# Sums, turns and products of a fused attention and highway layer, moved into two 64-row halves of the array

## The chip, the cores and the metric

The kernel runs on one core of a Trainium2 chip. The core has a matrix engine (TensorE, PE in the profile), VectorE (DVE), ScalarE (ACT), GpSimd (POOL) and SyncE (SP), which here only issues transfers; 16 DMA engines move data between HBM and the on-chip memory SBUF. TensorE writes its results into PSUM, eight banks of 512 fp32 columns on 128 partitions; VectorE and ScalarE read and write PSUM, GpSimd works on SBUF alone. The metric is the device time of one launch in microseconds: a median of 118.66 us over two runs (118.6 and 118.73) for the kernel before.

## The reference

q, k and v have the shape 8 batches x 8 heads x 576 positions x 64. Per batch and head

    q_s = exp(q) / sum of exp(q) over the 64 features      (per position)
    k_s = exp(k) / sum of exp(k) over the 576 positions    (per feature)
    x   = q_s @ (k_s^T @ v)                                (576 x 64)

The maxima that the reference takes off before exp cancel in the quotients. The eight heads side by side make x a matrix of 4608 rows and 512 columns, and a highway layer follows:

    H   = max(x @ w_h, 0)
    T   = 1 / (1 + exp(-(x @ w_t + b_t)))
    out = T * H + (1 - T) * x

## The kernel before

**Tiles.** The output is made in 36 tiles of 128 rows. Of each two batches b and b+1 come nine: four tiles of b, four of b+1, and one that holds the last 64 rows of both (tiles 8, 17, 26 and 35). Tiles 0, 4 and 5 are worked in two halves of the heads (HALVED); tile 35 is the last (LAST), its gate is split into two pieces of 256 columns.

**Order of the work.** ORDER (line 16) is one list of steps, written out by hand, such as `xu_9_0` or `bw_7:A`. The loop at the end goes through it and calls one function for each step. Every engine runs its own instructions in the order of the list, and semaphores hold an instruction until its inputs are there and its buffer is free. A letter names the engine: A for ScalarE, D for VectorE, P for GpSimd; F is an exp over a whole batch. Loads and stores are issued on SP's queue, in the order of the list too; a load waits until its landing buffer (three for each of q, k, v) is free.

**Steps of a batch.** `k`, `v`, `q` load. `ek` and `eq` are the exp of k and q on ScalarE, `vc` the cast of v to fp16. `kv` (line 262) multiplies exp(k) with v in 64 x 64 pieces of the array, 72 matmuls of 65 columns for a pair of head groups; the 65th column is the sum of exp(k). `kr` takes its reciprocal, and `kn` (line 283) writes the normed product to kvb, two heads on the diagonal of a 128 x 130 block, zeros beside them, and a column of ones for each head, from which the sum over exp(q) comes. `qt` (line 310) turns exp(q) on TensorE in three groups, 8, 8 and 2 turns of 128 x 128, and `qc` copies them to SBUF; for batch 7 a DMA (`qd`) turns the two large groups.

**Steps of a tile.**

- `xu` (line 348): four matmuls of 130 columns with kvb give x before its division, and the sums of exp(q). For a tile of two batches they are eight, each on 64 columns of the array.
- `rs`, `x` (lines 367, 372): VectorE takes the reciprocals and divides.
- `xt` (line 379), `xe`: TensorE turns x in four turns of 128 x 128, VectorE or ScalarE copies it to SBUF.
- `bw` (line 394): the bias b_t goes into a PSUM bank of the gate, by a copy on ScalarE (A) or by a matmul with ones (no letter).
- `mt` (line 406), `mh` (line 414): four matmuls of 512 columns each, with w_t into the gate's bank and with half of w_h less the identity into the carry's bank.
- `th`: tanh of half the gate, on ScalarE. `dd`: VectorE takes max(-x/2, carry). `uu`: (tanh + 1) times that, on VectorE, or with P in two steps on GpSimd; then tanh writes to SBUF (LIFTED) and the gate's bank is free after it. `oo`: adds x, on GpSimd. `st`: stores.

The identity taken from w_h and the halves make this equal to T * H + (1 - T) * x.

**PSUM.** Two banks for gates (ps_t), two for carries (ps_g), two for xu and kv together (ps_x), one for qt (ps_q), one for xt and the filling matmuls at the start (ps_xt).

Of the kernel before, what the change touches and what calls it, by code (L numbers as in the profile page):

```python
# [18 lines left out]
w_t_2 kr_0_0 whd_0:P whd_2:P w_t_0 k_1_2 v_1_2 q_1_0 k_1_0 v_1_0 fill_5 q_1_4 kn_0_0 q_2_0 k_2_0 eq_0_2 xu_0_0 v_2_0  # L19
q_3_0 rs_0_0 whc_0:A x_0_0 k_3_0 fill_4 v_3_0 kv_0_1 fill_3 kr_0_1 kn_0_1 xu_0_1 rs_0_1 xu_1_0 rs_1_0 qt_0_1 x_1_0  # L20
fill_6 whd_3:P qc_0_1 xt_1_0 xu_3_0 qt_0_2 qc_0_2:A xe_1_0:D fill_1 rs_3_0 x_3_0 x_0_1 xt_3_0 xu_2_0 rs_2_0 x_2_0
wtc_2:P whc_2:A mh_1_0 wtc_0:P vc_1_3 ek_1_3 ek_1_2 vc_1_0 xe_3_0:D mh_3_0 dd_1 xt_0_1 xt_0_0 mt_1_0 xe_0_0:D mh_0_0
xe_0_1 dd_3 xt_2_0 mh_0_1 mt_0_1 th_1_0 xe_2_0:D dd_0 vc_1_2:A kv_1_1 uu_1_0 oo_1_0 eq_1_0 mt_0_0 th_0_0 ek_1_0 ek_1_1
kr_1_1 bw_3 qt_1_0 vc_1_1:A kn_1_1 qc_1_0 mt_3_0 xu_5_1 uu_0_0 mh_2_0 th_3_0 bw_2 rs_5_1 x_5_1 dd_2 xu_4_1 kv_1_0
kr_1_0 eq_1_1 rs_4_1 xt_5_1 mt_2_0 th_2_0 kn_1_0 bw_5 xe_5_1:D x_4_1 xu_5_0 mt_5_1 qt_1_1 eq_1_2 rs_5_0 x_5_0 xt_5_0
xu_4_0 bw_4:A uu_3_0:P oo_3_0 xe_5_0:D mh_5_1 rs_4_0 x_4_0 mh_5_0 xt_4_1 qc_1_1:A xt_4_0 xe_4_1:D dd_5 eq_2_0 xe_4_0:D
v_4_0 mt_5_0 th_5_0 xu_6_0 qt_1_2 rs_6_0 qc_1_2 oo_0_0 mt_4_1 mh_4_1 mh_4_0 uu_2_0:P x_6_0 mt_4_0 eq_2_1 xt_6_0 xu_8_0
uu_5_0 bw_6:A xe_6_0:D qt_2_0 rs_8_0 x_8_0 mh_6_0 oo_5_0 th_4_0 xt_8_0 dd_4 uu_4_0 xu_7_0 mt_6_0 ek_2_0:F rs_7_0
vc_2_2:A bw_8 xe_8_0:D mt_8_0 x_7_0 th_6_0 xt_7_0 th_8_0 oo_2_0 vc_2_0 kv_2_0 oo_4_0 qc_2_0 q_4_0 bw_7:A qt_2_1
qc_2_1:A dd_6 uu_6_0:P oo_6_0 eq_3_0:F xe_7_0:D kr_2_0 kn_2_0 mh_8_0 xu_9_0 rs_9_0 x_9_0 mt_7_0 th_7_0 bw_9 dd_8  # L30
uu_8_0:P qt_2_2 qc_2_2:A xu_10_0 bw_10:A xt_9_0 xe_9_0:D rs_10_0 x_10_0 ek_3_0 mh_7_0 dd_7 ek_3_2 mh_9_0 xu_12_0 k_4_0
xt_10_0 k_5_0 rs_12_0 qt_3_0 xe_10_0:D x_12_0 mt_9_0 th_9_0 uu_7_0:P q_4_9 dd_9 xu_11_0 qc_3_0 vc_3_2:A xt_12_0
mt_10_0 rs_11_0 mh_10_0 x_11_0 v_5_0 q_5_0 vc_3_0 st_1_1 q_5_9 uu_9_0 dd_10 oo_7_0 kv_3_0 qt_3_1 th_10_0 oo_8_0 st_1_0
xe_12_0 bw_12:A mh_12_0 kr_3_0 qc_3_1:A kn_3_0 xu_14_0 rs_14_0 x_14_0 bw_11:A xt_11_0 xe_11_0 mt_12_0 th_12_0 qt_3_2
v_6_0 xt_14_0 oo_9_0 k_6_0 xu_13_0 q_6_0 xe_14_0 mh_11_0 dd_12 qc_3_2 mt_11_0 rs_13_0 eq_4_0:F th_11_0 uu_12_0
uu_10_0:P x_13_0 dd_11 xu_15_0 rs_15_0 vc_4_0 mh_14_0 x_15_0 st_5_1 dd_14 qt_4_0 oo_10_0 vc_4_2 xu_16_0 rs_16_0 x_16_0
xt_13_0 xe_13_0:D oo_12_0 bw_14:A bw_13:A ek_4_0:F st_3_0 mt_14_0 th_14_0 xu_17_0 rs_17_0 bw_15:A x_17_0 qc_4_0
xt_15_0 mt_13_0 kv_4_0 xe_15_0:D kr_4_0 uu_11_0:P oo_11_0 th_13_0 qt_4_1 uu_14_0:P st_3_1 mh_13_0 vc_5_2 xt_16_0
kn_4_0 mh_15_0 xe_16_0:D vc_5_0 xu_18_0 ek_5_0:F dd_13 xt_17_0 qc_4_1:A uu_13_0 xe_17_0:D dd_15 rs_18_0 oo_14_0
bw_16:A mt_15_0 mh_16_0 x_18_0 th_15_0 uu_15_0:P mt_16_0 dd_16 mh_17_0 oo_13_0 bw_17:A th_16_0 oo_15_0 kv_5_0 uu_16_0  # L40
kr_5_0 kn_5_0 oo_16_0 eq_4_2 dd_17 qt_4_2 xt_18_0 eq_5_0 mt_17_0 st_5_0 xe_18_0 xu_20_0 rs_20_0 mh_18_0 qc_4_2:A
bw_18:A q_7_0 th_17_0 mt_18_0 eq_5_1 bw_20:A uu_17_0:P x_20_0 xt_20_0 dd_18 vc_6_2 xe_20_0:D xu_21_0 th_18_0 rs_21_0
# [23 lines left out]
def kernel(  # L66
# [40 lines left out]
    b32 = consts.tile([P, DM], FP32, name="b32")  # L107
# [28 lines left out]
    def halves(b, k):  # L136
        return (k, k + 1) if b < 2 else (0, 2)
# [396 lines left out]
```

## Time and profile before

| | |
|---|---|
| median of the runs | 118.66 us |
| profiled execution, first to last instruction (span) | 116.9 us |
| TensorE busy | 109.5 us (94%), granted clock 0.995 |
| VectorE busy | 93.3 us (80%) |
| ScalarE busy | 90.0 us (77%) |
| GpSimd busy | 89.1 us (76%) |
| moved by DMA | 40.58 MB, 347 GB/s over the span |

The profile is of one execution. Of its time outside the span nothing is recorded; the median of the runs, 118.66 us, lies 1.8 us above the span, and that is taken for what lies around it. Busy time counts an engine's own instructions. Matmuls are pipelined, and their recorded ends are modelled, so what a matmul costs in a row is read from start to start. A group of instructions has a line of the kernel (L361 is line 361), an engine, what it writes and reads, the piece of the array in rows x columns for TensorE (128*64), the shape, its count, its busy time in us and the mean of one in ns. PEld is the loading of weights, which overlaps the matmuls.

### The profile page before, as it was taken

What the parts mean: (1) busy time and instruction counts of PE and PEld (TensorE: products, weight loads), DVE (VectorE), ACT (ScalarE), POOL (GpSimd) and SP (SyncE); (2) the same over time, 40 slices, a digit from 0 to 9 for tenths busy, and PEclk for the clock granted to TensorE, in tenths of its full rate; (3) what the DMA queues carried; (4) which work ended last, traced back from release to release, by engine and by line L of the source; (5) the groups of instructions that cost most, each with busy time, mean ns of one, the idle gap of its engine ahead of it and who ended that gap; (6) DMA issues with size and microseconds to landing.
All of it is one profiled execution on the core that took longest, in us unless ns stands there. A gap on an engine that the chain in (4) does not pass through costs nothing.

```text
span 116.9 us, 3424 instructions
## 1 busy us (share of the span) xinstructions
PE 109.5 (94%) x1351; PEld 61.6 (53%) x1351; DVE 93.3 (80%) x222; ACT 90.0 (77%) x132; POOL 89.1 (76%) x99
## 2 busy tenths in 40 slices
PE   5999987999999999999999999999999999999930
PEld 2354544545665656565665547566564555554520
DVE  5642587589799979979889798988989887899870
ACT  4356461897999999989999999998597998545520
POOL 5022237208996999999999999999989699999960
PEclk9999999999999999999999999999999999999998
DMA  2999999999999999999999999999999956992875
GB/s 42 399 392 377 408 398 385 375 377 379 393 391 397 383 391 393 358 375 387 357 376 360 387 392 363 390 381 383 399 398 217 302 204 270 397 404 115 315 295 179
DMA packets 24195, 40.58 MB, mean 347 GB/s; under 512 B 5362, under 2 KB 11762, under 8 KB 24180
## 3 DMA queue, kind: packets, MB, share of 16 engines
q1 hardware_dynamic: 24032, 40.24, 96.9%
q8 instruction: 10, 0.16, 0.6%
q10 hardware_dynamic: 148, 0.14, 0.4%
q14 instruction: 5, 0.04, 0.1%
HBM read 30.41 MB, written 9.44 MB: 341 GB/s over the span
## 4 chain that ended last, share of the span: by engine, by line
PE 67%; POOL 15%; issue 6%; DVE 5%; DMA 3%; SPq 1%; POOLq 0%; DVEq 0%
PE tps L411 18%; PE gps L419 16%; PE turned L167 9%; POOL o L471 7%; PE xu L361 6%; PE turned L384 5%; PE kv L269 5%; PE qps L324 4%; POOL u L451 4%; DMA out_dram<-o 3%; POOL g L450 2%; PE qps L319 2%; POOL v L259 2%; DVE x L376 2%; PE tps L401 1%
## 5 line engine op out<-in xcount | busy, mean ns | idle before, releaser
L471 POOL TENSOR_TENSOR o<-u,x 128x512 f32<-128x512 f16 (+1 forms) x36 | 40.6, 1143 | 1.6 <-DVE u L453 0.7
L411 PE MATMUL tps<-w16t,xT 128*128 128x512 f16 (+1 forms) x148 | 37.3, 373 | 0.0
L419 PE MATMUL gps<-w16h,xT 128*128 128x512 f16 x144 | 36.8, 379 | 0.5 <-DVE xT L391 0.5
L376 DVE TENSOR_TENSOR x<-xu,rs 128x512 f16<-128x512 f32 (+1 forms) x39 | 25.2, 649 | 2.4
L259 POOL CAST v<-v 128x1152 f16<-128x1152 f32 (+1 forms) x14 | 14.0, 1010 | 14.7 <-DMA v<-in_v_dram 13.7
L439 DVE SCALAR_TENSOR_TENSOR d<-x,gps 128x512 f16<-128x512 f16 x36 | 24.5, 680 | 0.3
L451 POOL TENSOR_TENSOR u<-g,d 128x512 f16<-128x512 f16 x17 | 19.7, 1158 | 1.7 <-DVE rs L370 0.4
L253 ACT ACTIVATE ek<-k 128x576 f16<-128x576 f32 (+2 forms) x15 | 17.9, 1225 | 3.0 <-DMA k<-in_k_dram 3.0
L419 PEld LDWEIGHTS <-xT 128*128 128x128 f16 x144 | 13.0, 98 | 12.3 <-DVE xT L391 1.8
L399 ACT COPY tps<-ball 128x512 f32<-128x512 f32 x28 | 16.6, 597 | 3.5 <-DVE u L453 3.2
L411 PEld LDWEIGHTS <-xT 128*128 128x128 f16 x148 | 13.2, 98 | 10.6 <-DVE xT L391 0.4
L361 PE MATMUL xu<-kvb,eq 128*128 128x130 f16 (+1 forms) x160 | 14.8, 224 | 0.2 <-DVE kvb L287 0.2
L384 PE MATMUL turned<-idh,x 128*128 128x128 f16 x144 | 14.2, 220 | 0.5 <-DVE x L376 0.5
L391 DVE COPY xT<-turned 128x512 f16<-128x512 f16 (+1 forms) x28 | 10.9, 391 | 4.2 <-PE turned L384 3.0
L435 ACT ACTIVATE tps<-tps 128x512 f32<-128x512 f32 (+1 forms) x20 | 11.2, 559 | 3.6 <-PE tps L411 3.3
L453 DVE SCALAR_TENSOR_TENSOR u<-tps,d 128x512 f16<-128x512 f32 (+1 forms) x19 | 12.7, 671 | 1.4 <-ACT tps L435 0.6
L361 PEld LDWEIGHTS <-eq 128*128 128x128 f16 (+1 forms) x160 | 10.0, 100 | 7.3 <-DVE x L376 2.5
L167 PE MATMUL turned<-blank 128*128 128x512 f16 x40 | 12.4, 458 | 1.5 <-POOL blank L149 1.3
L384 PEld LDWEIGHTS <-x 128*128 128x128 f16 x144 | 9.8, 98 | 6.0 <-DVE x L376 2.1
L307 ACT ACTIVATE qe<-q 128x1024 f16<-128x1024 f32 (+3 forms) x9 | 9.4, 1052 | 4.1 <-DMA q<-in_q_dram 4.1
L450 POOL TENSOR_SCALAR g<-th 128x512 f16<-128x512 f16 x17 | 10.6, 621 | 0.9 <-ACT th L433 0.9
L433 ACT ACTIVATE th<-tps 128x512 f16<-128x512 f32 x17 | 10.0, 594 | 0.9 <-PE tps L411 0.9
(48 smaller groups left out, 106.8 us busy)
## 6 DMA issues: line engine op xcount, KB each, us to landing
k<-in_k_dram SPq DMA_DIRECT2D x6, 1152.0 KB, 12.2
v<-in_v_dram SPq DMA_DIRECT2D x6, 1152.0 KB, 12.0
out_dram<-o SPq DMA_DIRECT2D x23, 256.0 KB, 4.0
q<-in_q_dram SPq DMA_DIRECT2D x10, 512.0 KB, 11.5
out_dram<-o SPq DMA_DIRECT2D x6, 512.0 KB, 3.8
k<-in_k_dram SPq DMA_DIRECT2D x4, 576.0 KB, 9.3
q<-in_q_dram SPq DMA_DIRECT2D x2, 1152.0 KB, 14.2
q<-in_q_dram SPq DMA_DIRECT2D x2, 640.0 KB, 10.5
```

What stands on the lines that cost most here:

```text
L167: nc.tensor.matmul(spare, blank[:, 0:P], blank, start=True, stop=True, skip_group_check=True)
L253: nc.scalar.activation(t[:, :, c:c + n].rearrange("p j c d -> p c j d"), T[f"k32{b}"][:, c:c + n].rearrange("p c (j d) -> p c j d", j=NJ), ...
L259: copy(v16[b % NV][:, c:c + n, :, 0:D], T[f"v32{b}"][:, c:c + n].rearrange("p c (j d) -> p c j d", j=NJ))
L361: nc.tensor.matmul(dst, turned_q(b, jp, n), kvb[b % NKV][:, hh, kk], start=True, stop=True, skip_group_check=True)
L376: nc.vector.tensor_mul(t[:, k0:k1], sums(i, k)[:, :, :, 0:64], T[f"rs{i}_{k}"][:, 0:k1 - k0].unsqueeze(3).to_broadcast([P, k1 - k0, 4, D]))
L384: nc.tensor.matmul(t[:, n], T[f"x{i}"][:, n0 + n % 2:n0 + 2 * P:2], idh, is_transpose=True, start=True, stop=True, skip_group_check=True)
L399: nc.scalar.copy(t[:, cs], ball[:, cs])
L411: nc.tensor.matmul(T[gate(i, k)][:, cs], T[f"xT{i}"][:, n], w16["t"][:, n, cs], start=False, stop=(n == parts[-1] and not first), skip_gro ...
L419: nc.tensor.matmul(t, T[f"xT{i}"][:, n], w16["h"][:, n], start=(first and n == parts[0]), stop=(n == parts[-1] and not (first and len(part ...
L439: nc.vector.scalar_tensor_tensor(t, T[f"x{i}"], -0.5, T[f"gps{i}"], op0=ALU.mult, op1=ALU.max)
L451: nc.gpsimd.tensor_mul(t, g, T[f"d{i}"])
L471: eng.tensor_add(t[:, cs], T[f"u{i}_{h}"][:, cs], T[f"x{i}"][:, cs])
```

## The change

From tile 9 on, and for q from batch 3 on, TensorE works in two halves of 64 rows, the upper with its own weights and its own PSUM bank, the lower likewise.

- `xu`: eight matmuls of 64 rows and 65 columns, one for each head, in place of four with zeros in half of the block. The normed product goes to kvl, without zeros; `kn` is then one instruction. A tile of two batches has sixteen.
- `xt` and `qt`: 64 x 64 identities, eight and sixteen (or four) turns of 64 rows and 64 columns, halves in different banks.
- `mm_i_0` and `mm_i_1` replace `mt` and `mh` of tiles 9 to 34: the gate's product is in one half of the array while the carry's is in the other, eight matmuls of 64 rows and 512 columns each; the second step swaps the halves. A drain of TensorE stands ahead of the second, as both halves add up in the same two banks.
- PSUM: xu, kv, qt and xt share two pairs of banks, given out by the order of the list.
- `bw` has a third form (D), a copy by VectorE.
- ORDER is new from its third line on. GpSimd has 24 `uu` (17 before), VectorE nine `bw` (none), ScalarE 22 `bw` (28), TensorE six (nine). Of the casts of v, ScalarE has ten (five), VectorE four (one), GpSimd six (fourteen). VectorE has 16 `qc` (10), ScalarE six (12); of `xe` VectorE has 26 (28), ScalarE 13 (11). Loads and stores are the same, in another order.

The diff, cut:

```diff
 ORDER = """
...
-kr_5_0 kn_5_0 oo_16_0 eq_4_2 dd_17 qt_4_2 xt_18_0 eq_5_0 mt_17_0 st_5_0 xe_18_0 xu_20_0 rs_20_0 mh_18_0 qc_4_2:A
-bw_18:A q_7_0 th_17_0 mt_18_0 eq_5_1 bw_20:A uu_17_0:P x_20_0 xt_20_0 dd_18 vc_6_2 xe_20_0:D xu_21_0 th_18_0 rs_21_0
...
+vc_5_0:A rs_20_0 x_20_0 mm_18_1 xu_21_0 rs_21_0 dd_18 th_18_0 mm_19_0 ek_6_0:F uu_17_0:P oo_17_0 x_21_0 xt_20_0
...
+xt_22_0 v_6_0 xe_22_0 mm_21_0 mm_21_1 uu_20_0 bw_22:A xu_24_0 x_23_0 dd_21 th_21_0 bw_23:D xt_23_0 st_16_0 eq_4_2
...
+dd_22 oo_18_0 xe_24_0:D mm_23_1 st_12_1 rs_25_0 q_7_0 x_25_0 kv_6_0 qt_4_2 th_22_0 dd_23 bw_24:A th_23_0 mm_24_0
+kr_6_0 kn_6_0 uu_23_0 qc_4_2:A xu_30_0 q_7_9 rs_30_0 eq_7_1 st_12_0 xt_25_0 xe_25_0:D mm_24_1 st_8_0 v_7_0 qt_6_0
...
+xu_27_0 mm_25_1 oo_22_0 xe_30_0 rs_27_0 x_27_0 xu_26_0 xt_27_0 rs_26_0 th_25_0 k_7_0 mm_30_0 xe_27_0:D xu_29_0 oo_23_0
...
+xu_28_0 dd_30 rs_29_0 x_29_0 ek_7_0:F mm_26_0 qd_7_0 st_23_0 xt_29_0 dd_27 xe_29_0:D uu_24_0:P rs_28_0 oo_25_0 eq_6_2
...
 """
...
-    ps_x = pool("ps_x", 1, space=PS)
-    ps_q = pool("ps_q", 1, space=PS)
-    ps_xt = pool("ps_xt", 1, space=PS)
+    ps_s = pool("ps_s", 1, space=PS)
...
-    kvb = [consts.tile([P, 2, 2, 130], FP16, name=f"kvb{i}") for i in range(NKV)]
+    kvb = [consts.tile([P, 2, 2, 130], FP16, name=f"kvb{i}") for i in range(2)]
+    kvl = [consts.tile([P, 2, 2, 66], FP16, name=f"kvl{i}") for i in range(NKV)]
...
+    EARLY, EARLY_Q = 9, 3
...
+    users = [pair_user(s) for s in ORDER.split()]
+    final = {u: n for n, u in enumerate(users) if u}
+    PAIR, held = {}, [None, None]
+    for now, u in enumerate(users):
+        if u and u not in PAIR:
+            free = [n for n in range(2) if held[n] is None or final[held[n]] < now]
+            PAIR[u] = min(free, key=lambda n: -1 if held[n] is None else final[held[n]])
+            held[PAIR[u]] = u
+    space = [ps_s.tile([P, 2, DM], FP32, tag=f"s{i}", name=f"space{i}") for i in range(2)]
+    space = {u: space[n] for u, n in PAIR.items()}
+    spare = space["early"][:, 1]
...
+    def setup_late(e):
+        for i in range(NKV):
+            nc.gpsimd.memset(kvl[i][:, :, :, 0::65], 1.0)
...
-        ps = once(f"kvps{b}", lambda: ps_x.tile([P, 2, DM], FP32, tag="xu", name=f"kv_{b}"))
+        ps = T[f"kvps{b}"] = space[f"kv{b}"]
...
+        if b >= 2:
+            nc.vector.tensor_mul(kvl[b % NKV][:, :, :, 1:65], kv_of(b, k)[:, :, :, 0:64],
+                                 T[f"rz{b}_{k}"].unsqueeze(3).to_broadcast([P, 2, 2, 64]))
+            return
...
+    def qt_late(e, b, g):
+        t = T[f"qps{b}_{g}"] = space[f"qt{b}_{g}"].bitcast(FP16)
+        for n in range(8 if g < 2 else 2):
+            for r in range(2):
+                rows = slice(64 * r, 64 * r + 64)
+                dst = t[:, r, 64 * n:64 * n + 64]
+                if g == 2:
+                    src = T[f"qe{b}"][rows, 8, 2 * n:2 * n + 2].rearrange("p c d -> p (c d)")
+                elif b in WIDE:
+                    main = T[f"qe{b}"].rearrange("p j c d -> p (j c d)")[:, 0:MAIN]
+                    main = main.rearrange("p (hh j kk f) -> p j hh kk f", j=4, hh=2, kk=2)
+                    src = main[rows, 2 * g + n // 4, n % 2, n % 4 // 2]
+                else:
+                    src = T[f"qe{b}"][rows, 4 * g + n // 2, n % 2 * 2:n % 2 * 2 + 2].rearrange("p c d -> p (c d)")
+                    dst = t[:, r, 0:512].rearrange("p (a k t s u) -> p a k s t u", a=2, k=2, s=2, u=2)[:, n // 2 % 2, n % 2, n // 4]
+                nc.tensor.matmul(dst, src, idh[rows, rows], is_transpose=True, start=True, stop=True,
+                                 skip_group_check=True)
...
-        t = T[f"qps{b}_{g}"] = ps_q.tile([P, a, 4, s * NP], FP16, tag="qps", name=f"qps_{b}_{g}")
-        if b in WIDE and g < 2:
...
+        if b >= EARLY_Q:
+            qt_late(e, b, g)
+            return
+        t = T[f"qps{b}_{g}"] = space["early"][:, 0].bitcast(FP16)[:, 0:a * 4 * s * NP].rearrange("p (a n t) -> p a n t", a=a, n=4)
...
-        copy(t.rearrange("p a n t -> p (a n t)"), T[f"qps{b}_{g}"].rearrange("p a n t -> p (a n t)"))
         T[f"eq{b}_{g}"] = t
+        if b < EARLY_Q:
+            copy(t.rearrange("p a n t -> p (a n t)"), T[f"qps{b}_{g}"].rearrange("p a n t -> p (a n t)"))
+        elif b in WIDE and g < 2:
+            copy(t.rearrange("p a n (r t) -> p r (a n) t", r=2),
+                 T[f"qps{b}_{g}"][:, :, 0:DM].rearrange("p r (m t) -> p r m t", m=8))
+        else:
+            m = 4 if g < 2 else 2
+            copy(t.rearrange("p a (k r) t -> p r (a k) t", r=2),
+                 T[f"qps{b}_{g}"][:, :, 0:m * s * NP].rearrange("p r (m t) -> p r m t", m=m))
...
-            t = ps_x.tile([P, 2, DM], FP32, tag="xu", name=f"xu_{i}")
+            t = space[f"xu{i}"]
...
+        if i >= EARLY:
+            for n in range(4):
+                kk, hh = n // 2, n % 2
+                for a, b in enumerate(bs):
+                    for w in range(2):
+                        part = slice(64 * w, 64 * w + 64)
+                        rows = slice(0, P) if len(bs) == 1 else slice(64 * a, 64 * a + 64)
+                        nc.tensor.matmul(t[rows, w, 65 * n:65 * n + 65], turned_q(b, jp, n)[part],
+                                         kvl[b % NKV][part, hh, kk, hh:hh + 65],
+                                         start=True, stop=True, skip_group_check=True)
+            return
...
+        if i >= EARLY:
+            nc.vector.reciprocal(t.rearrange("p w (k h) -> p w k h", k=2), pairs(i)[:, :, :, 0::129])
...
+        if i >= EARLY:
+            nc.vector.tensor_mul(t.rearrange("p k (w h) e -> p w k h e", w=2),
+                                 pairs(i)[:, :, :, 1:129].rearrange("p w k (h e) -> p w k h e", h=2),
+                                 T[f"rs{i}_0"].rearrange("p w (k h) -> p w k h", k=2).unsqueeze(4)
+                                 .to_broadcast([P, 2, 2, 2, D]))
+            return
...
-        t = T[f"xtps{i}"] = turned[:, 0]
+        if i >= EARLY:
+            t = T[f"xtps{i}"] = space[f"xt{i}"].bitcast(FP16)
+            for n in range(4):
+                n0 = n // 2 * 2 * P
+                for r in range(2):
+                    rows = slice(64 * r, 64 * r + 64)
+                    nc.tensor.matmul(t[:, r, 64 * n:64 * n + 64], T[f"x{i}"][rows, n0 + n % 2:n0 + 2 * P:2],
+                                     idh[rows, rows], is_transpose=True, start=True, stop=True,
+                                     skip_group_check=True)
+            return
+        t = T[f"xtps{i}"] = space["early"][:, 1].bitcast(FP16).rearrange("p (a n t) -> p a n t", a=2, n=4)[:, 0]
...
+        if i >= EARLY:
+            copy(t.rearrange("p n (r t) -> p r n t", r=2),
+                 T[f"xtps{i}"][:, :, 0:4 * NP].rearrange("p r (n t) -> p r n t", n=4))
+            return
...
-        bank = (ps_t, "tps") if i < LAST or h == 0 else (ps_q, "qps")
-        t = T[gate(i, h)] = bank[0].tile([P, DM], FP32, tag=bank[1], name=f"tps_{i}_{h}")
+        if i < LAST or h == 0:
+            t = T[gate(i, h)] = ps_t.tile([P, DM], FP32, tag="tps", name=f"tps_{i}_{h}")
+        else:
+            t = T[gate(i, h)] = space["last"][:, 0]
         cs = columns(i, h)
         if e == "A":
             nc.scalar.copy(t[:, cs], ball[:, cs])
-        else:
-            nc.tensor.matmul(t[:, cs], ones, b16[:, cs], start=True, stop=False, skip_group_check=True)
+        elif e == "D":
+            nc.vector.tensor_copy(t[:, cs], ball[:, cs])
+        else:
+            part = slice(0, P) if i < EARLY or i == LAST else slice(0, 64)
+            nc.tensor.matmul(t[:, cs], ones[part], b16[part, cs], start=True, stop=False, skip_group_check=True)
...
+    BY_PRODUCT = {int(s.split("_")[1]) for s in ORDER.split() if s.startswith("bw_") and ":" not in s}
+
+    def mm(e, i, r):
+        carry = once(f"gps{i}", lambda: ps_g.tile([P, DM], FP32, tag="gps", name=f"gps_{i}"))
+        low, high = slice(0, 64), slice(64, P)
+        if r == 1:
+            nc.tensor.drain()
+        for n in range(4):
+            two = [(T[gate(i, 0)], "t", (low, high)[r], False), (carry, "h", (high, low)[r], r == 0 and n == 0)]
+            for t, w, part, first in two[::-1] if i in BY_PRODUCT else two:
+                nc.tensor.matmul(t, T[f"xT{i}"][part, n], w16[w][part, n], start=first, stop=(r == 1 and n == 3),
+                                 skip_group_check=True)
...
```

More of the change, by code (lines that the diff above doesn't have):

```diff
@@ L157, in setup_dve @@
         nc.vector.memset(ones[32:33], 1.0)
-        for i in range(NKV):
+        for i in range(2):
             nc.vector.memset(kvb[i], 0.0)
@@ L360, in xu @@
                 dst = t[rows, kk - k0, 0:260].rearrange("p (s e) -> p s e", s=4)[:, hh:hh + 3:2]
[L361 removed]
+                nc.tensor.matmul(dst, turned_q(b, jp, n), kvb[b][:, hh, kk],
                                  start=True, stop=True, skip_group_check=True)
```

109 lines of the change are left out of this document (56 added, 53 removed).

## The prediction

> **What bounds the kernel now.** I read the page's engine line first, then the busy time by stretches of ten microseconds, then TensorE's instructions in order of time.
>
> ```profile
> PE 109.5 (94%) x1351; PEld 61.6 (53%) x1351; DVE 93.3 (80%) x222; ACT 90.0 (77%) x132; POOL 89.1 (76%) x99
> ```
>
> ```profile
> 0.00:10.00 10.00, 8.69 (x49) 3.59 (x52) 4.88 (x20) 4.67 (x7) 2.27 (x10) 1.00 0.84 291
> 10.00:20.00 10.00, 8.71 (x131) 4.80 (x128) 6.97 (x20) 4.98 (x7) 4.47 (x7) 1.00 1.04 394
> 20.00:30.00 10.00, 10.00 (x136) 5.16 (x134) 7.83 (x22) 8.28 (x14) 4.07 (x6) 1.00 1.07 378
> ...
> 60.00:70.00 10.00, 10.00 (x136) 5.44 (x134) 8.62 (x19) 9.34 (x14) 9.79 (x11) 1.00 1.07 378
> ...
> 100.00:110.00 10.00, 10.00 (x73) 5.30 (x72) 9.28 (x21) 5.31 (x11) 9.36 (x10) 1.00 0.75 292
> ```
>
> In the second view the columns after the length are TensorE, its weight loads, VectorE, ScalarE, GpSimd, the granted clock, the DMA share and GB/s. Up to 20 us the kernel waits for its inputs; from there TensorE is busy 10.00 of 10. A busy TensorE can still hide waits, because recorded ends are modelled, so its starts have to be read:
>
> ```profile
> 57.38 0.42 PE L361 MATMUL xu<-kvb,eq 128*64 128x130 f16 x8
> 57.74 0.40 PE L384 MATMUL turned<-idh,x 128*128 128x128 f16 x4
> 57.98 1.03 PE L411 MATMUL tps<-w16t,xT 128*128 128x512 f16 x4
> 59.00 0.77 PE L269 MATMUL kv<-v,ek 64*64 64x65 f16 x72
> 59.71 0.62 PE L319 MATMUL qps<-idh,qe 128*128 128x128 f16 x8
> 60.16 1.03 PE L419 MATMUL gps<-w16h,xT 128*128 128x512 f16 x4
> 61.03 0.39 PE L384 MATMUL turned<-idh,x 128*128 128x128 f16 x4
> 61.25 1.03 PE L419 MATMUL gps<-w16h,xT 128*128 128x512 f16 x4
> ```
>
> From start to start: eight turns of q take 0.45 us (59.71 to 60.16), four products 0.87 (0.216 each), four turns of x 0.22 (0.056 each). Nothing stands between them, so from 20 us to its last matmul near 112 us TensorE's own work is the length, some 92 us for 36 tiles, 2.55 us a tile. GpSimd (9.79 of 10) and ScalarE (9.34) are nearly as full, and VectorE (8.62) not far off. A shorter TensorE therefore meets the next limit soon.
>
> **The change, part by part: TensorE.** One group here already runs in pieces of the array: kv, 64 rows by 64 columns, four pieces at once. Its 72 matmuls start from 59.00; the last is recorded to end at 59.77, and one lasts 0.193 (row below), so it starts at 59.58. That is 71 steps in 0.58 us, 8.2 ns each, 33 ns for a round of four. I take 33 ns also for a pair in two row halves with 64 or 65 columns to stream.
>
> ```profile
> 37.52 0.22 PE tps L401
> ...
> 70.45 0.23 PE xu L361 x4
> ```
>
> - Sums (xu): 24 tiles from 9 on with one batch go from 0.23 to 4 pairs, 0.13: 24 x 0.10 = **2.4 us** saved. The three tiles of two batches (17, 26, 35) took 0.36 for eight and keep a change of array form on both sides: 0.2 together.
> - Turns of x (xt): 27 tiles from 0.22 to 0.13: **2.4 us**.
> - Turns of q (qt): batches 3 to 6, eight groups from 0.45 to 8 pairs, 0.26: 1.5; five small groups from two turns to two pairs: 0.2. Together **1.7 us**.
> - Bias by TensorE (bw without a letter): seven whole ones become four, the two half ones stay: 3 x 0.22 = **0.65 us**.
> - Products (mm): 8 pairs of 512 columns replace 8 matmuls of 512. A pair costs one stream, 0.216, if its halves run side by side: no gain, no loss.
>
> Sum saved: 2.4 + 0.2 + 2.4 + 1.7 + 0.65 = **7.35 us**.
>
> The drain is added once a tile for tiles 9 to 34, 26 times. No drain stands in the middle of this trace; two rows bound it. Leaving kv, the array changes its form by itself: last start 59.58, next 59.71, 0.13 in place of 0.03. [...] The other end is the DRAIN that TensorE's sequencer runs at the end of the program:
>
> ```profile
> L529 PEldq DRAIN  x2: 13/1074/2135, 110.0 to 116.5; - x2
> ```
>
> ```profile
> 111.05 1.04 PE L411 MATMUL tps<-w16t,xT 128*128 128x256 f16 x8
> ```
>
> The long one began at 110.0 and lasted 2.135, so it ended at 112.135, 0.045 after the last matmul's recorded end at 112.09. A product is recorded for 0.38 (1.03 less three steps of 0.216) and followed after 0.216; a drain would expose the 0.16 between, 0.045 of its own, and some 0.03 (estimate from the few hundredths between a weight load and its matmul) to fill up again: **0.24**. I take 0.24, since it is the same instruction: 26 x 0.24 = **6.2 us**; by 0.10 it would be 2.6, and 0.30, were refilling three times as long, 7.8. Behind the drain stands everything later on TensorE: the second half's eight matmuls, the next sums and turns, and with them VectorE's rs, x and xe, which can only start later.
>
> TensorE's sum: -7.35 + 6.2 = **-1.1 us**.
>
> **The other engines** get other shares of the work:
>
> ```profile
> L451 POOL TENSOR_TENSOR u<-g,d 128x512 f16<-128x512 f16 x17 | 19.7, 1158 | 1.7 <-DVE rs L370 0.4
> L399 ACT COPY tps<-ball 128x512 f32<-128x512 f32 x28 | 16.6, 597 | 3.5 <-DVE u L453 3.2
> ...
> L453 DVE SCALAR_TENSOR_TENSOR u<-tps,d 128x512 f16<-128x512 f32 x18 | 12.3, 685 | 1.3 <-ACT tps L435 0.6
> L259 POOL CAST v<-v 128x1152 f16<-128x1152 f32 x10 | 11.3, 1147 | 1.0 <-PE tps L411 0.9
> L253 ACT ACTIVATE ek<-k 128x2304 f16<-128x2304 f32 x5 | 10.6, 2122 | 0.0
> L450 POOL TENSOR_SCALAR g<-th 128x512 f16<-128x512 f16 x17 | 10.6, 621 | 0.9 <-ACT th L433 0.9
> ...
> L433 ACT ACTIVATE th<-tps 128x512 f16<-128x512 f32 x17 | 10.0, 594 | 0.9 <-PE tps L411 0.9
> ...
> L269 PE MATMUL kv<-v,ek 64*64 64x65 f16 x576 | 6.6, 193 | 0.0
> ...
> L333 ACT COPY eq<-qps 128x1024 f16<-128x1024 f16 x6 | 6.1, 1009 | 0.4 <-PE qps L324 0.3
> ...
> L333 DVE COPY eq<-qps 128x1024 f16<-128x1024 f16 x8 | 5.5, 684 | 1.6 <-PE qps L324 1.6
> ...
> L287 DVE TENSOR_TENSOR kvb<-kv,rz 64x256 f16<-64x256 f32 x12 | 5.1, 424 | 0.3
> ```
>
> - GpSimd: uu with :P goes from 17 to 24, 7 x (1.158 + 0.621) = +12.5; eight casts of v of 1.147 leave, -9.2; one cast of weights leaves, -1.0; three memsets of 8 columns come, between nothing and, by the nearest row, three casts of 1152 columns, 3.4: at their size 0.3. Together +2.6: 89.1 to 91.7.
> - VectorE: seven uu leave, -4.8; six qc come, +4.1; six kn at 0.424 leave, -2.5; one whole and two half casts of v come, +2.3 at GpSimd's rate; two xe leave, -0.8; nine biases (bw:D) come, a form that the trace hasn't, between 0.424 and 0.685, the nearest rows: 0.6 each, +5.4. Together +3.7: 93.3 to 97.0.
> - ScalarE: six biases leave, -3.6; six qc leave, -6.1; seven whole casts of v come and two halves go, +6.8 at GpSimd's rate; one weight cast, about the size of a qc, +1.0; two xe, the size of a bias, +1.2. Together -0.7: 90.0 to 89.3.
>
> By 20 us VectorE has done 11.9 and GpSimd 6.7. What is left, 85.1 and 85.0, has to fit beside TensorE's 91 us. It does, at 94%, which full stretches above reach. So I cost these at nothing; TensorE's stream is the cover. If TensorE fell below some 88 us, that cover would be gone.
>
> Loads and stores are the same in bytes, but their steps move on SP's queue: the load of q for batch 7 has to wait for the last exp of q of batch 4 (its buffer), which now stands about 10 us of TensorE's steps later in the list; v and k of batch 7 follow behind it and behind four stores. The DMA share is over 1.0 in the stretches shown up to 70 us, so nothing lands sooner than its bytes allow: 3.5 MB of loads and 1.05 MB of stores at 378 GB/s take 12 us. From that exp to the first user of k TensorE's steps in the list add up to 15 us: covered, with 3 us to spare. The first exp of q itself comes 6 us after its buffer is free, and its 1.05 MB take 2.8: also 3 us to spare. Were they late, ScalarE would stand still at that exp, with bias and tanh queued behind it.
>
> **The sum** is made on the profiled execution, a span of 116.9 us; the median of the runs is 118.66, 1.8 more for what lies around the span. 116.9 - 1.1 + 1.8 gives **117.5 us**.
>
> **The rivals.**
>
> 1. *The drain is as cheap as a change of form* (0.10). TensorE saves 7.35 - 2.6 = 4.8, to 87 us, and GpSimd's 85.0 us at 9.79 of 10 need the same 87. That gives **114 us**. [...] Against it: the sequencer's DRAIN was recorded to outlast the matmul's full end.
>
> 2. *The two gate banks bind, and the kernel is slower.* A gate bank is held from its bias to the end of tanh. Before, that was 0.60 + 0.87 + 0.16 + 0.59 = 2.2 us, of 2 x 2.55 = 5.1 that two banks give. Now it is held through both halves and the drain: 0.60 + 1.73 + 0.24 + 0.16 + 0.59 = 3.3, so bias and tanh may stand 1.8 us in ScalarE's queue and no longer. One exp of k lasts 2.12, and ten casts of v instead of five stand there too, 1.15 each. It decides where both come between: 2.12 + 1.15 - 1.8 = 1.5 us of an idle TensorE, of which sums and turns of other tiles fill perhaps 0.5. At one such place for each of batches 3 to 7, 5 x 1.0 = 5 us: **122.5 us**. For it: the carry bank is opened at the same moment, and both end together. Against it: nine biases are on VectorE, and 24 gates leave their bank with tanh.
>
> 3. *The halves don't gain*, because a weight load of 128 columns, not the 64 columns streamed, sets the pace. The nearest row for such loads is a full turn, 0.056. Then sums and turns cost what they did, the drains come on top, -0.65 + 6.2 = +5.5: **124 us**. Against it: full turns hide such loads already, and in kv eight instructions fit into 33 ns. [...]
>
> **How the numbers follow.** A time within 2% of 118.66, from 116.3 to 121.0, is about what a measurement of this kernel can't tell from no change. Forecast 0.41, its own range 115.5 to 119.5 (VectorE's and GpSimd's fill costs up to 2 us above, a drain of 0.17 gives 2 below), a fifth of it under 116.3. Rival 1: 0.25. Rival 2: 0.26, of which a tenth ends below 121. Rival 3: 0.08. Faster: 0.25 + 0.08 = 0.33. Slower: 0.23 + 0.08 = 0.31, same 0.36. Leaving out a tenth on each side, the range goes from 113.8 to 123.
>
> **What would show it.** Start to start: four sums and four turns each near 0.13; a drain's gap between a tile's two product halves, 0.46 instead of 0.22, 26 times; and TensorE without other gaps. Rival 1 shows that gap near 0.32 and GpSimd ending the chain; rival 2 shows the first product of a tile waiting for ScalarE's or VectorE's bias; rival 3 shows sums at 0.22. I would be wrong if the halves of a product take turns instead of running side by side (pairs at 0.43), or if batch 7's loads come late by more than those 3 us.

## The result, and the profile after

The changed kernel takes **132.47 us** (median of two runs, 132.32 and 132.62), against 118.66: a ratio of 1.116, with a 95% interval from 1.112 to 1.120. The forecast was 117.5 us in a range from 113.8 to 123.0, so the change is slower by 13.8 us, and the range missed it by 9.5.

From the page of the changed kernel, the engine line, then the granted clock and the DMA share in 40 slices of 3.3 us, then the queue by which instructions are brought in (packets, MB, share):

```profile
span 130.6 us, 4481 instructions
...
PE 110.3 (84%) x1858; PEld 58.2 (45%) x1858; DVE 96.0 (74%) x222; ACT 90.6 (69%) x128; POOL 91.8 (70%) x107
...
PEclk9999995999999999999999999999959999999997
DMA  3999999999999999999978999999509302997274
...
q8 instruction: 14, 0.23, 0.7%
```

VectorE, ScalarE and GpSimd came out where the prediction put them (97.0, 89.3 and 91.7 forecast). TensorE is busy for as long as before, but only 84% of a longer span: it stands still. The clock falls in two slices, which it did not before. The busy time by stretches, in the columns known from the prediction, shows where:

```profile
10.00:20.00 10.00, 7.30 (x88) 4.14 (x89) 5.66 (x17) 5.63 (x8) 3.57 (x9) 0.98 1.04 394
20.00:30.00 10.00, 9.59 (x96) 4.82 (x97) 7.11 (x16) 6.71 (x12) 3.32 (x5) 0.85 1.07 382
30.00:40.00 10.00, 7.99 (x101) 4.66 (x102) 6.78 (x19) 6.91 (x11) 8.05 (x9) 1.00 1.05 390
...
60.00:70.00 10.00, 9.62 (x234) 5.38 (x230) 9.22 (x22) 9.57 (x12) 9.47 (x11) 1.00 0.90 317
70.00:80.00 10.00, 7.60 (x140) 4.25 (x142) 7.98 (x19) 8.43 (x11) 9.52 (x11) 1.00 1.05 382
...
90.00:100.00 10.00, 7.77 (x178) 4.08 (x171) 6.23 (x14) 6.21 (x10) 5.67 (x6) 0.83 0.51 162
```

Two different stretches are bad: 10 to 40 us, before any half is used (the first starts at 45.7), and 70 to 100 us. The starts of the carry's VectorE step `dd` say the same. The first is at 19.5 us before and 23.4 after, the tenth at 46.2 and 53.3, the last at 111.4 and 124.8: about 7 us are lost by the tenth tile and 6 behind it.

The view of TensorE's waits (who waited for whom, us in total, times, longest) names the two kinds:

```profile
PE space L465 <- issue: 2.6, 2, 2.0
PE space L299 <- issue: 2.5, 2, 2.0
PE space L472 <- DVE eq L382: 1.4, 2, 0.8
...
PE space L371 <- DVE xT L483: 0.9, 1, 0.9
...
PE space L197 <- DVE eq L382: 0.4, 1, 0.4
```

Turns of x (L472) and filling matmuls (L197) wait for VectorE's copy of turned q (eq), turns of q (L371) for the copy of turned x (xT). Neither needs the other's data; they only write into the same pair of banks (`space`). "Issue" is a wait that no semaphore explains. In TensorE's timeline one of the two longest lies inside one group of eight turns:

```profile
71.91 0.38 PE L530 MATMUL tps<-w16t,xT 64*128 64x512 f16 x1
71.93 0.38 PE L530 MATMUL gps<-w16h,xT 64*128 64x512 f16 x1
72.12 0.28 PE L465 MATMUL space<-idh,x 64*128 64x64 f16 x7
74.41 0.20 PE L465 MATMUL space<-idh,x 64*128 64x64 f16 x1 [2.00 <-issue]
```

The eighth turn is of the same step as the seven before it, reads the same tile and writes into the same pair of banks, and starts over 2 us later.

### The profile page after: what moved, and what is told of

Read it like the earlier page. It is cut to its first block, busy times and chain, and to the rows that moved or that the text cites. A ratio compares the mean times of both kernels' runs of the same rounds, so it can differ in the third digit from the quotient of the medians.

```text
span 130.6 us, 4481 instructions
## 1 busy us (share of the span) xinstructions
PE 110.3 (84%) x1858; PEld 58.2 (45%) x1858; DVE 96.0 (74%) x222; ACT 90.6 (69%) x128; POOL 91.8 (70%) x107
## 4 chain that ended last, share of the span: by engine, by line
PE 73%; issue 9%; DVE 7%; POOL 5%; ACT 3%; POOLq 1%; DVEq 0%
PE tps L530 30%; PE space L197 8%; PE tps L508 6%; PE gps L516 5%; PE gps L530 5%; PE space L299 5%; POOL o L582 3%; PE space L465 3%; PE space L418 3%; PE space L472 3%; DVE eq L382 3%; PE space L359 2%; PE space L371 2%; DVE xT L483 1%; PE space L427 1%
## 5 line engine op out<-in xcount | busy, mean ns | idle before, releaser
L530 PE MATMUL tps<-w16t,xT 64*128 64x512 f16 x208 | 54.1, 382 | 2.7
L530 PE MATMUL gps<-w16h,xT 64*128 64x512 f16 x208 | 54.2, 383 | 0.0
L562 POOL TENSOR_TENSOR u<-g,d 128x512 f16<-128x512 f16 x24 | 27.7, 1155 | 3.6 <-DVE d L550 1.7
L530 PEld LDWEIGHTS <-xT 64*128 64x128 f16 x416 | 17.8, 95 | 21.1 <-issue 9.4
L449 DVE TENSOR_TENSOR x<-space,rs 128x512 f16<-128x512 f32 x27 | 18.4, 685 | 1.3 <-POOL o L582 0.5
L197 PE MATMUL space<-blank 128*128 128x512 f16 x40 | 12.0, 447 | 2.6 <-POOL blank L145 1.3
L516 PE MATMUL gps<-w16h,xT 128*128 128x512 f16 x40 | 11.5, 405 | 0.0
L289 ACT CAST v<-v 128x1152 f16<-128x1152 f32 (+1 forms) x10 | 10.9, 1097 | 0.1
L508 PE MATMUL tps<-w16t,xT 128*128 128x512 f16 (+1 forms) x40 | 10.2, 370 | 0.4 <-DVE xT L483 0.4
L465 PE MATMUL space<-idh,x 64*128 64x64 f16 x216 | 8.2, 193 | 2.6 <-issue 2.6
```

The lines of the kernel that those rows point to most:

```text
L197: nc.tensor.matmul(spare, blank[:, 0:P], blank, start=True, stop=True, skip_group_check=True)
L289: copy(v16[b % NV][:, c:c + n, :, 0:D], T[f"v32{b}"][:, c:c + n].rearrange("p c (j d) -> p c j d", j=NJ))
L449: nc.vector.tensor_mul(t.rearrange("p k (w h) e -> p w k h e", w=2), pairs(i)[:, :, :, 1:129].rearrange("p w k (h e) -> p w k h e", h=2), ...
L465: nc.tensor.matmul(t[:, r, 64 * n:64 * n + 64], T[f"x{i}"][rows, n0 + n % 2:n0 + 2 * P:2], idh[rows, rows], is_transpose=True, start=True, ...
L508: nc.tensor.matmul(T[gate(i, k)][:, cs], T[f"xT{i}"][:, n], w16["t"][:, n, cs], start=False, stop=(n == parts[-1] and not first), skip_gro ...
L516: nc.tensor.matmul(t, T[f"xT{i}"][:, n], w16["h"][:, n], start=(first and n == parts[0]), stop=(n == parts[-1] and not (first and len(part ...
```

## Two theories

**A, shared banks.** The early qt, and the early xt with the filling matmuls, were two tiles of one bank. Now they are one tile of two banks, and a step on one bank waits for a step on the other. This would be the loss up to 40 us.

**B, late instruction blocks.** There are four such stops, at 72.21, 80.91, 86.72 and 92.68 us, with gaps between starts of 2.20, 0.67, 0.81 and 2.19 us, 5.8 in all beyond the usual steps. Counted in all that TensorE's records hold (weight loads, matmuls, drains, waits for semaphores), the instruction behind each is

```
changed kernel      1987   2241   2497   2753
less 193, over 256  7.01   8.00   9.00  10.00
```

So they lie 256 instructions apart; the 193 is fitted to them. Each packet of the instruction queue has 16,384 bytes (0.23 MB in 14). Packets start at 71.97, 79.19, 85.15 and 92.34 us, and TensorE goes on 2.4 to 2.5 us behind each. These four packets start 3.6 to 4.8 us behind the edge before theirs; the next three, when the DMA share has fallen (0.26 from 100 to 110 us), start 1.1 to 2.2 us behind it. That fits a block of 256 instructions that is fetched through the DMA engines, late while these are full (a share of 0.95 to 1.08 from the edge to the packet at the four). No packet of this kernel starts ahead of the edge before its own. The changed kernel has 507 matmuls more than before and as many loads, 38 more for each of 27 tiles on some 72; from 41 us on it uses a block up in 4.3 to 7.3 us (stops left out), the kernel before in 7.2 to 11.9.

Rival to both: the new order of the steps, and the drains, make up the loss.

## The experiments

Experiments 7 and 8 were run four times, the others once. Each time stands beside runs of the kernel before on the same chip: 118.8 us in the first four, 119.0 in the next three, 119.1 in the last two.

**1. The shared pair alone.** The kernel before, with qt up to batch 2 and xt up to tile 8 in one tile of two banks; nothing else is changed.

```diff
+    pair = shared.__enter__().tile([P, 2, DM], FP32, tag="early", name="pair")
+    spare = pair[:, 1]
...
+        if b < 3:
+            t = pair[:, 0].bitcast(FP16)[:, 0:a * 4 * s * NP].rearrange("p (a n t) -> p a n t", a=a, n=4)
...
+        if i < 9:
+            t = pair[:, 1].bitcast(FP16).rearrange("p (a n t) -> p a n t", a=2, n=4)[:, 0]
```

> The kernel before, with one thing of the change alone: up to tile 8 and batch 2 the turned q and the turned x (and the filling matmuls) lie in the two banks of one PSUM tile in place of two tiles. Theory A (steps that use different banks of one tile wait for each other, and that costs the changed kernel 3.9 us by its first carry and 7.1 us by its tenth): the first carry's VectorE step comes at 22 to 24 us in place of 19.5, and the whole takes 123 to 126 us. Rival (the new order of the early steps costs it, not the tile): within 1 us of the kernel before, 118 to 120.

125.52 us, 6.7 more. The first `dd` comes at 21.8 us, a little ahead of the 22 to 24 expected, and the tenth at 53.0 (19.5 and 46.2 before); behind that the two kernels run side by side. VectorE's and TensorE's waits in this run:

```profile
DVE eq L344 <- PE pair L174: 4.2, 2, 3.4
...
DVE xT L406 <- ACT eq L344: 2.4, 2, 1.2
```

```profile
PE pair L399 <- ACT eq L344: 1.1, 1, 1.1
...
PE pair L399 <- DVE eq L344: 0.8, 1, 0.8
```

The copy of turned q waits for filling matmuls (L174) in the other bank. **Theory A holds**: in before's order the sharing costs 6.7 us.

**2. The changed kernel without that sharing.** Its early pair becomes two tiles of one bank each, and one pair again from tile 9 on.

```diff
+    bank_q = ps_e.tile([P, DM], FP32, tag="eq", name="early_q")
+    bank_x = ps_e.tile([P, DM], FP32, tag="ex", name="early_x")
...
-        t = T[f"xtps{i}"] = space["early"][:, 1].bitcast(FP16).rearrange("p (a n t) -> p a n t", a=2, n=4)[:, 0]
+        t = T[f"xtps{i}"] = bank_x.bitcast(FP16).rearrange("p (a n t) -> p a n t", a=2, n=4)[:, 0]
```

> The changed kernel, with the turned q and the turned x of the early part in two PSUM tiles of one bank each. Theory A: the first carry's VectorE step back from 23.4 to about 20 us, the clock not halved at 19.6 us, the whole 4 to 7 us shorter: 125.5 to 128.5. Rival (new order): 131.5 to 133.

129.29 us: 3.2 less than the changed kernel, and less of a gain than expected. The tenth `dd` comes at 48.5 us instead of 53.3, the last at 121.5 instead of 124.8: 4.8 us are won early, and 1.5 given back later. The granted clock accounts for part of both. The changed kernel has a stretch of 3.41 us at half clock (0.50) at 19.57 us, which this run hasn't, and behind 70 us this run has two of them, the changed kernel one; each is worth an estimated 1.7 us at most, half its length. So the split by itself wins about 3.1 us. The waits for "issue" are still there:

```profile
PE space L482 <- issue: 2.5, 2, 1.9
PE space L316 <- issue: 2.0, 2, 1.7
```

The stops now come at other times, behind the instructions 1473, 1985, 2499 and 2754, which are again 193 to 195 above a multiple of 256. Three of these are the same edges as before, within two instructions, and so the same steps of the list. That alone can't tell the count of instructions from the work at that place; the next experiment can.

**3. More instructions alone.** The kernel before, with each product of 512 columns of tiles 9 to 34 cut into four of 128. The same columns are multiplied, with 48 TensorE instructions more a tile.

```diff
+        if 9 <= i < LAST:
+            for n in parts:
+                for c in range(0, DM, P):
+                    nc.tensor.matmul(T[gate(i, k)][:, c:c + P], T[f"xT{i}"][:, n], w16["t"][:, n, c:c + P], start=False,
...
```

> The kernel before, with each product of tiles 9 to 34 cut into four matmuls of 128 columns: 48 more instructions a tile on TensorE, the same work, order and layout. Their stream is 4 x 56 in place of 216 ns, 1.7 us in all. Theory B (TensorE waits at the edge of a block of 256 instructions whose transfer is late, since the DMA engines are full): idle stretches of 0.5 to 2.2 us that lie 256 instructions apart, 4 to 8 us of them, so 124 to 128 us. Rival (the count of instructions costs nothing): 118.7 + 1.7 = 120.4.

126.71 us, 7.9 more, with no half, no drain, and before's banks and order. TensorE's timeline:

```profile
72.14 0.50 PE L413 MATMUL tps<-w16t,xT 128*128 128x128 f16 x6
74.92 0.72 PE L413 MATMUL tps<-w16t,xT 128*128 128x128 f16 x10 [2.27 <-issue]
```

Its three long stops (1.7, 2.5 and 1.8 us) stand behind the instructions 1730, 2241 and 2754, 193 or 194 above a multiple of 256, in a stream that is another one than the changed kernel's. They are 5.9 us of the 7.9; 1.7 is the slower stream of the pieces (4 x 0.056 in place of 0.216). **Theory B holds**: instructions alone bring the stops.

**4. Drains alone.** The kernel before, with a drain ahead of `mh` of tiles 9 to 34.

```diff
+        if 9 <= i < LAST:
+            nc.tensor.drain()
```

> The kernel before, with a drain of TensorE ahead of the carry's product of tiles 9 to 34, 26 drains and nothing else. At 0.27 us each, as the gaps in the changed kernel show, and with TensorE as the limit throughout: 118.7 + 7.0 = 125.7 us. At the 0.10 of a change of form: 121.3. If other engines' waits hide them: under 120.

126.05 us: 7.3 more, or 0.28 for each of 26. In its timeline:

```profile
63.04 0.39 PE L384 MATMUL turned<-idh,x 128*128 128x128 f16 x4
63.53 1.03 PE L421 MATMUL gps<-w16h,xT 128*128 128x512 f16 x4
```

Four turns and the drain behind them take 0.49 where four turns took 0.22. No "issue" stands among its matmuls' waits.

**5 and 6. The new order with the whole array.** The changed kernel with sums, turns and products on 128 rows again and without drains, so with before's number of instructions; and the same with the early pair split as in experiment 2.

```diff
-        if i >= EARLY:
+        if False:
...
-        carry = once(f"gps{i}", lambda: ps_g.tile([P, DM], FP32, tag="gps", name=f"gps_{i}"))
...
+        (mh if r else mt)(e, i, 0)
```

> The changed kernel with its new order of steps and its two shared pairs of banks, but with sums, turns and products on all 128 rows again and without the drains, so that TensorE has about 72 instructions a tile as before. Theory B (late instruction blocks) and the measured drain: the four stalls (5.8 us) and the 26 drains (some 7 us) go, and the 7 us that the halves had saved come back, so 125 to 127.5 us, with no stall of TensorE over 1 us that lies on an edge of 256 instructions. Rival (order and shared banks cost all of the 13.7 us, and halves, drains and blocks sum to nothing): 132.

> The run before (whole array, no drain) with the early pair split into two tiles of one bank each. The split alone was worth 3.2 us in e2_split_pair, with block stalls that took some of it, and the shared pair alone cost 6.7 us in e1_shared_pair. If shared pairs are all that is wrong with the new order: 118.7 to 120 us. If the new order of steps costs by itself: more, up to 124, and the difference to the kernel before is its price.

126.82 us (125 to 127.5 expected) and 123.79 us, and among the waits of neither's matmuls stands an "issue". So splitting the pair gains 3.0 here too. What is left of the change, the new order with its shares of the engines and its late pairs, costs 4.8, and 2.9 of that is lost by the tenth `dd` (49.1 us instead of 46.2). TensorE's waits in the second of them have several short entries that before's list doesn't have:

```profile
PE space L446 <- DVE kvb L338: 0.8, 3, 0.4
...
PE tps L518 <- ACT w16t L269: 0.4, 1, 0.4
PE tps L518 <- DVE xT L493: 0.4, 1, 0.4
```

All the time by which its starts lie further apart than is usual for their forms (only where that is over 60 ns) sums to 11.4 us, against 6.1 before; from 46 us on it is 3.6 against 0.8. Of these 3.6 us, 1.5 are four groups of sums waiting for VectorE's `kn` (kvb), 0.8 are turns of x waiting for x, and 0.3 are turns of q that wait for VectorE to read the x of a tile out of the banks that they write to. How much the list itself costs, and how much the two pairs that xu, kv, qt and xt share from tile 9 on, was not tried: the new list keeps the sums of two tiles open at once, which needs the two pairs, and before's list keeps qt, xt and xu open at once, which needs before's banks.

**7. Halves without drains.** As experiment 2, with sums, turns and bias in halves, but the products whole.

```diff
...
-        if r == 1:
-            nc.tensor.drain()
...
+        (mh if r else mt)(e, i, 0)
```

> The changed kernel with the early pair split, sums, turns and bias in halves, but the products on all 128 rows without a drain: about 96 TensorE instructions a tile instead of 112. Against e2_split_pair (129.3) the 26 drains go (7 us). If instruction blocks still come late at 96 a tile, about 3 to 5 us of stalls stay: 119 to 123 us. If they come in time: 115 to 118 us, faster than the kernel before, and the halves' gain of some 7 us is seen at last. Rival (the new order costs several us by itself): over 123.

121.39 us, a ratio to before of 1.021 (1.017 to 1.025). That is in the range named for late blocks, but for another reason: no stop over 0.6 us is left behind 23 us. TensorE's starts show the price instead. The piece of the array that is used changes in 112 places, in 28 before (at kv and at the tiles of two batches). From a product to a half 0.312 us pass from start to start instead of 0.216, and from a half to a whole matmul 0.122 instead of 0.03. So each change of form costs 0.095 us, and 84 more of them 8.0 us, a little more than the 7.35 that the halves save. Against experiment 6 the halves should then lose 0.6 us; they gain 2.4, to which I come back below.

**8. The smallest part alone.** The kernel before, with the sums from tile 9 on in halves; order, banks, turns and products are before's.

```diff
+        if i >= EARLY:
+            for n in range(4):
...
+                        nc.tensor.matmul(t[rows, w, 65 * n:65 * n + 65], turned_q(b, jp, n)[part],
+                                         kvl[b % NKV][part, hh, kk, hh:hh + 65],
...
```

> The kernel before with one part of the change alone: sums from tile 9 on in halves (pairs of matmuls on 64 rows, eight instead of four), with before's order of steps, before's PSUM banks, whole products, no drain, whole turns. If the halves gain what the terms say (2.4 us for the sums) and 80 TensorE instructions a tile are still supplied in time: 116 to 117.5 us, faster than the kernel before. If other engines or waits set the pace as soon as TensorE gets shorter: 118.2 to 119. If halves cost something between TensorE's groups: over 119.5.

120.89 us, a ratio of 1.015 (1.013 to 1.017): slower by 1.5%, small but clear of the noise, and the third of the cases named. Its timeline, and a stretch of before's:

```profile
87.73 0.39 PE L418 MATMUL turned<-idh,x 128*128 128x128 f16 x4
88.05 0.30 PE L374 MATMUL xu<-kvl,eq 64*128 64x65 f16 x8
88.28 1.04 PE L453 MATMUL gps<-w16h,xT 128*128 128x512 f16 x4
```

```profile
78.85 0.40 PE L361 MATMUL xu<-kvb,eq 128*128 128x130 f16 x4
79.08 1.02 PE L411 MATMUL tps<-w16t,xT 128*128 128x512 f16 x4
```

The sums still take 0.23 to the next start: four pairs fit into 0.13, and the change back takes the rest. The turns ahead of them take 0.32 instead of 0.22, for the change into halves. There are 76 changes of form instead of 28, two more for each of the 24 tiles of one batch: 48 x 0.095 = 4.6 us lost against 2.6 saved (2.4 and the 0.2 of the other tiles), 2.0 on balance, and 1.8 measured.

**9. Fewer bytes.** The changed kernel without the stores of tiles 0 to 25; that part of the output is left out.

```diff
+        if i < 26:
+            return
```

> The changed kernel without the stores of tiles 0 to 25 (that part of the output is left out), so that about 6.5 MB fewer pass through the DMA engines between 50 and 110 us. Theory B with the full DMA engines as the cause of the late blocks: the four stalls on edges of 256 TensorE instructions (together 5.8 us) fall to under 2 us and the time to 126 to 129 us. Rival (a block is late for another reason, whatever the DMA engines do): the stalls stay and the time is 131 to 133 us.

128.35 us. The stretches of this run:

```profile
60.00:70.00 10.00, 9.56 (x237) 5.45 (x236) 9.11 (x23) 9.45 (x12) 9.47 (x11) 1.00 1.06 381
70.00:80.00 10.00, 7.48 (x115) 3.89 (x113) 6.52 (x15) 6.97 (x9) 8.88 (x10) 0.83 0.50 165
80.00:90.00 10.00, 9.62 (x220) 5.19 (x216) 8.95 (x20) 8.99 (x13) 8.67 (x9) 1.00 0.97 340
90.00:100.00 10.00, 9.66 (x226) 5.36 (x228) 9.03 (x20) 8.78 (x15) 7.18 (x8) 1.00 0.29 57
```

```profile
PE space L465 <- issue: 2.2, 1, 2.2
```

Up to 70 us the DMA share is as full as it was (1.06 from 60 us on), and the stop at 70.66 us is still there (2.37 us). At the three edges behind it, the same instructions as in the changed kernel follow within 0.2 us of the one before, where 0.7, 0.8 and 2.2 us had stood. The packets of these three edges start 1.7 to 2.8 us behind the edge before, instead of 3.6 to 4.8. So with these stores gone the packets start sooner and the stops at these edges go; that a block is late because its transfer stands among the others is inferred from this. The stops fell by 3.5 us in sum, where I had expected 3.8 or more. The time fell by 4.1, but 1.7 of that is there by the tenth `dd` (51.6 us): this run has no early stretch at half clock.

## Why the prediction was wrong

Two steps failed. "TensorE's own work is the length" left out that the instructions have to arrive, which costs 5.8 us of stops. "So I cost these at nothing", said of the other engines, put nothing for the waits that the new order brings (4.8 us). The sum also has no term for the early pair of banks that qt and xt came to share (3.0). The terms of TensorE's own work came out within 0.8 us of their sum.

**What bounds the kernel.** "TensorE's own work is the length" was read rightly, but taken to hold for any stream of matmuls. That the instructions themselves have to arrive was no step of the prediction. This costs 5.8 us of stops. Behind the last of them the clock is granted at half for 3.41 us (94.67 to 98.08), worth an estimated 1.7 more at most; the other such stretch, at 19.57 us, lies ahead of any half.

**Sums, turns, bias.** The pace of 33 ns a pair was right: pairs start every 29 ns, and four sums take 0.13 from start to start, as forecast (60.42 to 60.55):

```profile
60.42 0.29 PE L418 MATMUL space<-kvl,eq 64*128 64x65 f16 x8
60.55 0.37 PE L530 MATMUL tps<-w16t,xT 64*128 64x512 f16 x1
...
61.41 0.30 PE L465 MATMUL space<-idh,x 64*128 64x64 f16 x8
61.82 0.38 PE L530 MATMUL tps<-w16t,xT 64*128 64x512 f16 x1
```

For sums and turns the saving is there as put (the bias's 0.65 was not read by itself). What experiments 7 and 8 add is that it is had only while everything beside them is in halves as well.

**Products.** A pair costs one stream: pairs start every 0.216 us, no gain and no loss, as put.

**The drain.** 0.24 us was close. The turns above end in a drain and take 0.41 instead of 0.13, so 0.28; behind a product, where nothing else waits, the gap is 0.457 to 0.465 (forecast 0.46), so 0.25. That makes 7.0 us for 26 instead of 6.2, within the bounds of 2.6 and 7.8. With that, TensorE's sum is -0.35 instead of -1.1: nothing is gained even where nothing goes wrong.

**The other engines, costed at nothing.** Their loads were right within 1.3 us each, but "it does, at 94%" was a statement on sums, and this was the step that failed for the order: experiment 6 loses 4.8 us, and its TensorE starts show 5.3 us more of short waits than before's, with every other engine at 81% or less.

**PSUM.** The prediction didn't price that qt and xt came to share a tile. That is 3.0 us by experiments 5 and 6, 3.2 by experiment 2.

**Batch 7's loads.** They were not late: behind 60 us no engine of the changed kernel waits for a load.

**Put together**, from 119.0 us: the new order and its late pairs +4.8 (experiment 6), the early pair +3.0 (experiment 5), everything with the halves +5.7 (132.47 less 126.82). Of the last, 1.5 us are not the halves': the early stretch at half clock, which experiment 5 hasn't, already puts the first `dd` at 23.4 us instead of 21.9. That leaves 4.2 us for the halves. By terms it is -7.35 for the work, +7.0 for drains, +5.8 for stops, +1.7 for the late clock, so 7.2: the terms are 3.0 too high. From experiment 6 to experiment 2 they are too high by 3.0 as well (-7.35 + 7.0 + 5.4 + 3.4 against the 5.5 measured), and so they are from experiment 6 to 7 (+0.6 against -2.4). In the first two, eight more changes of form (0.8) aren't counted yet.

So the halves bring a gain of about 3 us that no term has. For experiment 7 the trace shows most of it. The time between starts beyond what is usual is 7.6 us there, against 11.4 in experiment 6, and 0.8 against 3.6 from 46 us on. The four waits of sums for `kn` have gone. Without zeros in the block `kn` is one instruction in place of two; VectorE's rows in experiments 6 and 7 are

```profile
L338 DVE TENSOR_TENSOR kvb<-space,rz 64x256 f16<-64x256 f32 x12 | 5.1, 423 | 0.3
```

```profile
L333 DVE TENSOR_TENSOR kvl<-space,rz 128x256 f16<-128x256 f32 x6 | 2.6, 426 | 0.2
```

The prediction had this as 2.5 us less of VectorE's load, and took VectorE to be covered. That the shorter `kn` is what removes the waits is argued; no run changes `kn` alone. The early 2.9 us of the new order stay open.

**The rivals.** Rival 1 fell with the drain's price. Rival 2 (gate banks) did not happen: no product waits for a bias in the list of waits. Rival 3 fell with the 29 ns; a load of 128 columns before each half did not set the pace here. What came true, stops for instructions, a shared pair of banks and the short waits of the new order, was none of them, and neither sign that was named for being wrong appeared. So the range was too short on that side.

## What to carry to other kernels

Cutting matmuls into halves of the array pays only if the pieces saved outweigh the changes of form (0.095 us each way here) and any drains (0.25 to 0.28), so count the neighbours of a group as well as the group. Count instructions as well as work: in the changed kernel four blocks of 256 TensorE instructions, used up in 4.3 to 6.5 us, ended in a stop (3.6 to 4.8 us from the edge before to the packet, at a DMA share of 0.95 to 1.08, and 2.4 to 2.5 until TensorE went on); the kernel before, at 7.2 us and more, had none. The sign is a stop named "issue" inside a group, moving with the count of instructions. When two buffers become one PSUM tile (6.7 us in experiment 1), look for waits between steps that share no data.

## What the runs showed of the hardware

- In the changed kernel one packet of 16,384 bytes, of the instruction queue that the profile lists among the DMA queues, starts behind each of 14 edges of 256 TensorE instructions. The packets of the four stops start 3.6 to 4.8 us behind the edge before theirs, with a DMA share of 0.95 to 1.08 between the two; TensorE goes on 2.4 to 2.5 us later, after stops of 0.7 to 2.2 us. The next three start after 1.1 to 2.2 us, at a share of 0.00 to 0.32, and no stop follows; the last (117.01 us) starts after 1.0, at 1.08. Experiment 3 stopped for up to 2.5 us, at a share of 1.07 from 70 to 80 us. In experiment 9 none of these stops stands behind that at 70.66 us, at shares of 0.50, 0.97 and 0.29 in the three stretches of 10 us from 70 us on.
- After some stops of 2 us the clock was granted at half (0.50) for 3.41 us: in the changed kernel behind the stop of 2.19 us, in experiment 9 behind that of 2.37 (0.83 on average from 70 to 80 us), in experiment 2 behind stops of 2.12 and 1.92 (0.970 over the whole span). Behind other stops of that size it stayed at 1.00 (the changed kernel at 72.21, experiment 3 with 2.49, both 1.00 from 70 to 80 us); what decides it stays open. The changed kernel has a second such stretch, from 19.57 to 22.98 us, behind three early waits of about 1 us each (1.16, 1.14 and 0.85); experiments 5 and 9 have the same three waits and no such stretch.
- In experiments 7 and 8 a change between 128-row and 64-row pieces cost 0.093 to 0.096 us in either direction, whether a product or a turn stands ahead of it.
- A drain of TensorE ahead of a product cost 0.27 us in experiment 4, behind products and turns alike (0.486 instead of 0.216, 0.325 instead of 0.056).
